# A window-attention kernel: the first pair's key shift from half its keys, copies on ScalarE at the end, another order

## The chip, the cores and the metric

The kernel runs on one core of a Trainium2 chip. The core has a matrix engine (TensorE, PE in the profile, with its weight loads as PEld), VectorE (DVE), ScalarE (ACT), GpSimd (POOL) and SyncE (SP), which here only issues transfers. The matrix engine writes to PSUM, eight banks of 128 partitions x 512 floats; everything else lies in SBUF. The metric is the time of one execution on the device in microseconds; lower is better.

## The reference

x is an image of 224 x 224 positions with 96 channels. Queries, keys and values come from one product; the channels are then cut in two halves of 48. The first half attends within 28 horizontal stripes of 8 rows, the second within 28 vertical stripes of 8 columns, 1,792 positions each. The output product joins both.

```python
qkv = jnp.einsum('bhwc,cd->bhwd', x, wqkv)
q, k, v = (qkv[..., :C], qkv[..., C:2 * C], qkv[..., 2 * C:])
scale = C2 ** (-0.5)                                  # C2 = 48
qh = q[..., :C2].reshape(B * nh, sw * W, C2)          # kh, vh alike
ah = _softmax(jnp.einsum('bqc,bkc->bqk', qh, kh) * scale, axis=-1)
oh = jnp.einsum('bqk,bkc->bqc', ah, vh).reshape(B, H, W, C2)
# qv, kv, vv: the other half, x transposed into vertical stripes; ov alike
o = jnp.pad(oh, (..., (0, C2))) + jnp.pad(ov, (..., (C2, 0)))
return jnp.einsum('bhwc,cd->bhwd', o, wo)
```

So 56 stripes need 1,792 x 1,792 scores each, an exponential of each score, and a product with the values.

## The kernel before

Two stripes make a pair; 28 pairs are worked one after the other, 14 horizontal and then 14 vertical. One stripe of a pair lies on partitions 0 to 63 and the other on 64 to 127, so that their small products run side by side. A pair has four chunks of queries (512, 512, 512, 256) and 14 tiles of 128 keys. One tile is 128 keys x 512 queries of both stripes, 1,024 columns in two PSUM banks.

Most tiles are of kind A: PE makes the scores (`qk_fn`, line 697), ScalarE takes one exponential of 128 x 1024 (line 867), and PE multiplies with the values (`pv_fn`, line 723), adding up the chunk in one bank. There are 1,126 such tiles. They use two pairs of banks in turn, so the scores of a tile wait for the exponential two tiles before. The other 246 tiles (kinds P and R) get a polynomial exponential instead: PE makes a score product (line 710), DVE and POOL work on it, PE makes the product a second time, and DVE joins the two. The remaining four banks (`RING`) serve these, the sums, and the fills: small products for keys, queries and values of the next pair, and for the output.

Softmax doesn't change when all keys are shifted by one vector, and the kernel takes a mean key off every key to keep the scores in range. For the first pair that shift is made ahead: `t_lead` turns x with PE transposes, the evictions to SBUF add up each quarter's x on the way (`xs_sb`), `kb_fn` multiplies the sums with the key weights, `kb_d` makes the shift `kb_sb`, and the evictions of the first pair's keys (`k_ev`) add it. Later pairs do it through an extra column of the query weights.

The order is written out by hand, or rather found ahead of time: `ORDER` is a string for each pair, and every letter is one item of PE's program. `q` is the score of an A tile with its exponential on ScalarE (`do_q`), `v` a product with the values (`do_v`), `1` and `3` the first and `2` and `4` the second score of a polynomial tile (`do_s`), `k` a fill for a pair ahead, `g` an output product, `f` one of the last pair's final products (`do_fill`); `K` and `G` are two fills in one. The first letters run after the lead, which is laid out by `lead_pe` and `lead_ev`. A planner (`tm` and the constants at the head of the file) walks through the letters with assumed durations, and from its times it decides which DVE, POOL and DMA step goes next; PE and ScalarE follow the letters. `emit` then writes each engine's list with its semaphore waits. Every engine works its list in order.

Names that come up below: `spin` puts filler matmuls on a zero tile into PE's list up to a time; `NTWICE` makes the scores of the first tiles twice, as filler; `XR1` and `XR2` are the times at which the planner expects the transposed x of the second and third pair; `emit_ot` copies a chunk's sums to SBUF; `out_fills` are the output products of a pair (letter `g`), `fin_fills` those of the last pair (`f`: a product, a reciprocal of the sums and a multiply-add for each 96 columns, lines 611, 618 and 623); `store` sends finished rows to the output by the queue of SP, ACT or POOL, whichever is free first by the planner's account. The lead transposes for stripe w and half hf of x, in two quarters h2:

```python
for w, hf, bs in ((0, 0, (6, 7)), (1, 0, (2, 3)), (0, 1, (6, 7)), (1, 1, (2, 3))):
    for h2 in range(2):
        f = t_lead(w, hf, h2)
        lead_pe(f, bs[h2])
        lead_ev(f, bs[h2], 0, h2 == 1)      # True: evicted by ScalarE
```

Of the kernel before, what the change touches and what calls it, by code (L numbers as in the profile page):

```python
# [32 lines left out]
D_ST, D_SW, D_TAIL = 1.0, 0.60, 1.0  # L33
XR1, XR2, TURN = 19.5, 43.0, 4.5
# [5 lines left out]
NTWICE = 11  # L40
# [5 lines left out]
    "kkqqkkq3q3q3qkqkqkqkq1q1qvvq4qkvqkv4qkqvv1qkvqvqvvq4vqkvvqkvq1vqvvq1vkqvkq4vqkvq1vqv2qvkqkqvkq2vvq3qvvvqvkq2vqvvkq",  # L46
    "1qvvvqvq2vvq1qvvqvvq3vvqvvqvkqkvqvKqvvq4qvkvq2qvvq2vqv1qvvqvqv1qvvvq4qvkvq3qvkq2vqv2qvq3vqkvqvvqkq4vqvvq4vqkvq3vqkvvqk",
    "v2qvqv1qvvvvq1qvvvvqvq3vvqvq3kqqvvqvkq4vkqq2vkqv1qkvqvvq4qvkvq3qkvqvkq2qvvq4vqkvq1vvq2qvvkq2qvv1qvvqvvqkvqvvkq1vqv2qvvq",
    "1vq2qvvq1vvqvqvvvqv1qvq1vvqvqvq4qkvq1vqvvqvq2vqv1qvv4qkqvv1qvqvkq2vqkvvq2vkqvkq3vqkqvvvqv1qvq4vqkq3vqkvq4vqvkvq4vqkvq2vk",
    "qvq1vvqvvqv2qvq1vq2qvvvqv2qvvq1qvvvqvvq1qvvqvkvqvkq1qvkqvkvq4vqvvq1qv2qkvqkv1qvvqkvqq2vqkvq1qkvvq2qvvvq1qkkqvvq2vkqvv1",  # L50
    "qvqvvqv2qvvq1vvqvv1qvvqvqv2qq4vqvkq1vqvvvqvq1vqkvkqkvvq2kqv3qkvqv4qvvqkq1vqvvvqkqvv4qvqkv2qvvq2vqv1qvq4vqvvqkvkvq1qkvvq2v",
    "vq1qvvqvvq1vvqvq1vqvvqvv3qvvqvvqvkq2qv1qvqkv2qkvqvq2vvq1qkvvvq2kqq4vqvkq1vvqkqvvq4qkvqv1qvq4vkqvq3vkqvvq3qkvqvvqvvkvq",
    "2qvv1qvvq2vq3qvvqvvqvvq1vqvvvqkqvkvq1qvvkqv2qkvqv2qkvvq1vqv4qvkqvvq2vq4qvvkq1qvkvqvvqv2qvvq2qvv3qvkqv1qvvqkvq4vqvkvq4qvvvkq1",
    "qvvqvvq2vvqvvq1vq2qvvvq1qvvqvq1vkqvvqvkqvkqv2qkvqv2qkq1vqvvq2vqv2qvkvqkq1vqv1qvqvvvqv1qkqvvvq1qkvq2qvkqv2qvvvq1kqvvqk",
    "vqvvq2vvq4qvvvvq1vqvvq4qvkq1qvvqvvvq2vqv1qvvqvkqvkqvvvq2q1qvvq1vvqkvq2vkqv3qkvqvvqvqkq4vqkq3vqvvq4vqkvqk2qvvq1vqvvkq2qkv",
    "vq1vvqvqvvvqv2qvvq1vqvkqkvkqv4qvqvk1qkqvvqv2qvq1vkqvqvvvqv4qvqkq3vqkvq3vqvvq4vqkvq2vqv1qvvqkqvvvqv3qkvqv2qvq1vkqvq2vqv2",
    "qvv1qvqvvvqvv2qvq1vvq1qvvqv1qvqvvq3qvvqvkkqkvq4qkvqv4qkvqv2qvvqv2qvvq3vqvkq1qvvqvkq4qvkqv1qvvvq2qkvqv1qvv2qvkqvkvq2qvk",
    "vvq1qkvvvqvvqvq1vqv2qvvvq1qvvqvvq1qvvqv4qkqvv3qkvqkq2vqv4qvkqvq2vvq1qvv2qkqv3qvkqvvvqkvq4qkvvq4qvvvq1qkvqkvkq2qvvq1vkqvv",
    "1qvqvvvq1qvvq1vqvvqvvq2qvv2qq2vqvvkq1qvkvqvvqv3qqvk2qvvqkvq1qv2qvvqv1qkvqkvqvvq2vqv3qvkqv4qvkqv3qvvqkq2vvqkkqvkvq1qvv",
    "vqvq1vvq2qvvq2vqv2qvvvvq3qvvvkq4qvvkvq1qvvvvqvv1qkvqv2qvqkvvq2kqv1qvvqvvvq2qvkqkkvq4qkvvqv3qvkqvvq1vqv1qkvqvvqvkvvq2qvvq1vgvvqq2vvvq",  # L60
    "vv1qvq4vqvkqvkq1vqgvqvvqv4qvvkq2qvvq1vvkqv1qkvq2qvvkqvgvq2qvvgvq1qvvgqvvvqv1qvqkq4gqvgvq3qvkq4qvvgq1qkvqvvkqvqvkgqv2qvq2vqvkvv",
# [113 lines left out]
def bass_standalone__window_attn_cswin__vision_kernel(  # L175
# [10 lines left out]
    CA = C2 + 1  # L186
# [17 lines left out]
    with es:  # L204
# [15 lines left out]
        xs_sb = sb("xs_sb", [C, 2, 4], BF16)  # L220
        kbj = sb("kbj", [128, 4], FP32)
# [410 lines left out]
        def out_fills(P):  # L632
# [3 lines left out]
            for k0 in range(0, 2 * NKT, FS):  # L636
# [16 lines left out]
                fills.append(fill("B", D_G * n, pe_fn, ["wo6"] + [("ocT", b, y) for y in range(z + 1)],  # L653
                                  [(0.07 + 96 * n * 0.001026, d, [], ["add"] if last else [("og", b, k0)], None, st)],
# [84 lines left out]
        def t_lead(w, hf, h2):  # L739
# [8 lines left out]
            acc = xs_sb[0:C, w, 2 * hf + h2:2 * hf + h2 + 1]  # L748
# [6 lines left out]
            def d(e, bk):  # L755
                dst, src = views(bk)
                return e.tensor_scalar(dst, src, 1.0, None, ALU.mult, ALU.add, accum_out=acc)

            def da(e, bk):
                dst, src = views(bk)  # L760
                return e.activation(dst, src, ACTF.Copy, accum_out=acc)
            return fill("B", 0.21, pe_fn, [("x", w, hf), "ident"],
                        [(0.6, d, [], [("xT", 0, w, hf, h2), ("xs", w, hf, h2)], da)], [], ("T", 0, w, hf) + (() if h2 else (0,)))

        def kb_fn(e, bk):
            for w in range(2):
                ins = e.matmul(bk[64 * w:64 * w + 64, 0:4], lhsT=w_sb[0:C, wblk(0, "k"), :], rhs=xs_sb[:, w, :], start=True, stop=True)
            return ins

        def kb_d(e, bk):  # L770
            return e.tensor_scalar(kbj[:, :], bk[:, 0:4], -alpha / NTOK, None, ALU.mult, ALU.add, accum_out=kb_sb[:, :])
        HH = [(hf, h2) for hf in range(2) for h2 in range(2)]
        KB = fill("B", 0.07, kb_fn, ["w", "w0z"] + [("xs", w, hf, h2) for w in range(2) for hf, h2 in HH],
# [48 lines left out]
        spin(S.done[("dve", S.cnt["dve"] - 1)])  # L822
        spin(S.done[("dve", S.cnt["dve"] - 1)], 128)
# [41 lines left out]
        def emit_qk(tl, s, slot):  # L865
            S.commit("pe", 0.0, D_MM, L_MM, qk_fn(tl, s, 2 if 1 <= ia[0] <= NTWICE else 1), kt_keys(tl), set_keys(s), fresh=set_keys(s))
# [27 lines left out]
        def store(st, done):  # L894
            if st:
                for item in st[5]:
                    q = "sp"
                    if ia[0] >= len(act_seq):
                        tm["aq"] = max(tm["aq"], tm["act"])
                        if max(done, tm["aq"]) < max(done, tm["sp"]):  # L900
                            q = "aq"
                    if ip[0] == len(p_seq) and not pq and not nq and all(d["what"] != "rn" for d in dq):
                        tm["gq"] = max(tm["gq"], tm["pool"])
                        if max(done, tm["gq"]) + D_SW < max(done, tm[q]) + D_TAIL and i2[0] == len(p_seq):
                            q = "gq"
                    tm[q] = max(done, tm[q]) + (D_SW if q == "gq" else D_TAIL if st[5][0][0] in (NP - 2, NP - 1) else D_ST)
# [104 lines left out]
        tm = dict(pe=8.43, act=7.83, end=0.0, dve=8.74, pool=11.6, sp=0.0, aq=0.0, gq=0.0, mode="B", run=9, fin=False)  # L1011
        set_free = [8.05, 7.4]
        bank_free = dict(zip(RING, (8.89, 7.98, 6.3, 6.6)))
# [5 lines left out]
        k_t = {(0, 0): 8.6}  # L1019
        q_t = {(0, 0): 7.98}  # L1020
# [3 lines left out]
        x_t = {0: 7.4, 1: XR1, 2: XR2}  # L1024
# [200 lines left out]
        def do_q():  # L1225
# [7 lines left out]
            tw = D_MM if 1 <= ia[0] <= NTWICE else 0  # L1233
# [54 lines left out]
        def do_v():  # L1288
# [163 lines left out]
```

## Time and profile before

| what | value |
|---|---|
| runs | 1055.43, 1056.22, 1056.88 us (median 1056.22) |
| the profiled execution: time, span | 1057.54 us, 1055.7 us |
| PE busy | 1027.3 us (97%) |
| ACT busy | 1041.8 us (99%) |
| DVE busy | 1014.0 us (96%) |
| POOL busy | 985.1 us (93%) |

Span is the time from the first to the last instruction of the profile. In the rows, the first two numbers of a timeline row are the start in us from the span's start and the length of the merged instructions; then come engine, line, operation, what is written and read with shapes, and how many. What stands in brackets is idle time of the engine just before and what ended it. In a row of a group, the numbers after the bar are busy time and mean ns of one, and after the second bar the idle time before them with what ended most of it. `SPq`, `ACTq` and POOL's DMA rows are issues of transfers.

### The profile page before, as it was taken

The numbers are of one execution on the slowest core, as the hardware profiler recorded it, in microseconds if no ns is written. First come the engines' busy times: TensorE is split into PE (matmuls) and PEld (weight loads), VectorE is DVE, ScalarE is ACT, GpSimd is POOL, SyncE is SP. The second block draws the span as 40 slices with busy tenths as digits, with TensorE's granted clock in tenths as the row PEclk, the third lists the DMA queues.
The fourth block names the chain that finished last, engine by engine and source line by source line (L and its number), as shares of the span: only waits on it lengthen the run. The fifth ranks groups of instructions, "written<-read, shape, count | busy, mean of one in ns | idle before, by whom it ended". The sixth has DMA issues, their size and how long they took to land.

```text
span 1055.7 us, 32757 instructions
## 1 busy us (share of the span) xinstructions
PE 1027.3 (97%) x13456; PEld 385.9 (37%) x13456; DVE 1014.0 (96%) x1748; ACT 1041.8 (99%) x1137; POOL 985.1 (93%) x654
## 2 busy tenths in 40 slices
PE   9999999999999999999999999999999999999998
PEld 4333333333333333333333433434333333333343
DVE  7989999999999999999999999999999999999998
ACT  7999999999999999999999999999999999999997
POOL 7999999999988998999999999988999999999997
PEclk9999999999999999999999999999999999999999
DMA  9867527654752854222176545537634553674352
GB/s 191 171 133 140 102 51 145 112 96 89 141 94 56 143 104 74 36 59 55 30 77 92 81 91 101 92 52 109 96 64 82 88 91 67 101 100 52 66 75 69
DMA packets 413079, 96.84 MB, mean 92 GB/s; under 512 B 403648, under 2 KB 410016, under 8 KB 412928
## 3 DMA queue, kind: packets, MB, share of 16 engines
q1 hardware_dynamic: 412080, 93.66, 51.8%
q8 instruction: 105, 1.72, 0.7%
q0 software_dynamic: 448, 0.69, 0.2%
q10 hardware_dynamic: 400, 0.39, 0.1%
q14 instruction: 46, 0.38, 0.1%
HBM read 28.31 MB, written 28.21 MB: 54 GB/s over the span
## 4 chain that ended last, share of the span: by engine, by line
PE 54%; ACT 22%; DVE 10%; POOL 7%; issue 6%; DMA 0%; ACTq 0%; POOLq 0%; DVEq 0%
ACT PT L867 22%; PE ps L723 20%; PE ps L697 20%; PE ps L710 7%; DVE PT L994 3%; POOL PT L1002 3%; PE ps L530 3%; DVE qb L989 3%; POOL PT L1005 2%; PE ps L575 1%; POOL PT L1006 1%; PE ps L644 1%; DVE PT L991 1%; DVE og L650 1%; DVE V_sb L582 1%
## 5 line engine op out<-in xcount | busy, mean ns | idle before, releaser
L867 ACT ACTIVATE PT<-ps 128x1024 bf16<-128x1024 f32 x1126 | 1037.2, 1080 | 4.1 <-PE ps L697 2.9
L1002 POOL TENSOR_TENSOR PT<-PT 128x1024 f16<-128x1024 f16 x246 | 461.8, 1894 | 20.3 <-DVE PT L991 11.3
L697 PE MATMUL ps<-QT_sb,KT_sb 49*64 49x512 bf16 (+1 forms) x5332 | 461.6, 362 | 15.9 <-ACT PT L867 9.7
L723 PE MATMUL ps<-PT,V_sb 128*49 128x512 bf16 (+1 forms) x3136 | 464.4, 361 | 0.0
L994 DVE SCALAR_TENSOR_TENSOR PT<-ps,PT 128x512 uint16<-128x512 f32 (+1 forms) x405 | 312.4, 799 | 15.7 <-PE ps L710 6.8
L989 DVE TENSOR_SCALAR qb<-ps 128x512 f16<-128x512 int16 (+1 forms) x421 | 313.7, 775 | 11.9 <-PE ps L710 7.8
L1005 POOL TENSOR_TENSOR PT<-qb 128x1024 f16<-128x1024 f16 x150 | 283.2, 1894 | 22.9 <-DVE qb L989 10.8
L697 PEld LDWEIGHTS ps<-QT_sb,KT_sb 49*64 49x64 bf16 x5332 | 135.4, 104 | 308.3 <-ACT PT L867 284.2
L723 PEld LDWEIGHTS ps<-PT,V_sb 128*49 128x49 bf16 x3136 | 134.2, 103 | 205.7 <-issue 173.5
L710 PE MATMUL ps<-QT_sb,KT_sb 50*64 50x512 bf16 (+1 forms) x1968 | 196.6, 390 | 5.3 <-DVE PT L994 1.2
L1006 POOL TENSOR_SCALAR PT<-PT 128x1024 f16<-128x1024 f16 x150 | 156.9, 1046 | 12.8
L991 DVE SCALAR_TENSOR_TENSOR PT<-ps,qb 128x512 f16<-128x512 int16 (+1 forms) x172 | 123.0, 743 | 0.2
L710 PEld LDWEIGHTS ps<-QT_sb,KT_sb 50*64 50x64 bf16 (+1 forms) x1968 | 55.8, 103 | 76.3 <-DVE PT L994 22.9
L884 DVE CAST OT_sb<-ps 113x512 bf16<-113x512 f32 x112 | 68.9, 615 | 0.5 <-PE ps L723 0.4
L544 DVE CAST QT_sb<-ps 128x512 bf16<-128x512 f32 (+1 forms) x111 | 67.0, 614 | 1.7 <-PE ps L530 1.0
L535 DVE TENSOR_SCALAR_CACHE_REDUCE KT_sb<-ps 128x512 bf16<-128x512 f32 x106 | 63.8, 617 | 1.3 <-PE ps L530 0.8
L650 DVE CAST og<-ps 128x480 bf16<-128x480 f32 x84 | 51.4, 617 | 1.4 <-PE ps L644 0.7
L582 DVE CAST V_sb<-ps 128x480 bf16<-128x480 f32 (+1 forms) x84 | 51.3, 616 | 0.4 <-PE ps L575 0.4
L530 PE MATMUL ps<-xT_sb,w_sb 97*64 97x512 bf16 x224 | 41.9, 371 | 0.3 <-DVE qb L989 0.2
L530 PE MATMUL ps<-xT_sb,wq_sb 97*64 97x512 bf16 x224 | 40.8, 367 | 0.1
L575 PEld LDWEIGHTS ps<-w_sb,xT_sb 96*64 96x64 bf16 x1568 | 33.5, 112 | 16.1 <-issue 7.1
L575 PE MATMUL ps<-w_sb,xT_sb 96*64 96x48 bf16 x1568 | 39.1, 190 | 0.0
(66 smaller groups left out, 248.6 us busy)
## 6 DMA issues: line engine op xcount, KB each, us to landing
xT_sb<-xt_dram SPq DMA_DIRECT2D x28, 336.0 KB, 5.2
xp_dram<-in_x_dram SPq DMA_DIRECT2D x26, 336.0 KB
oc_all<-xp_dram SPq DMA_DIRECT2D x26, 336.0 KB, 3.6
xt_dram<-xT_sb SPq DMA_DIRECT2D x26, 336.0 KB, 6.5
out_dram<-og SPq DMA_DIRECT2D x181, 48.0 KB, 2.0
oh_all<-ohn SPq DMA_DIRECT2D x52, 84.0 KB, 2.8
stg<-oh_all SPq DMA_DIRECT2D x13, 336.0 KB, 6.0
xt_dram<-xT_sb SPq DMA_DIRECT2D x4, 168.0 KB, 4.6
```

What stands on the lines that cost most here:

```text
L530: ins = e.matmul(bk[64 * w:64 * w + 64, 0:qs], lhsT=lw, rhs=xT_sb[b][0:C + 1, w, q0:q0 + qs], start=True, stop=True)
L575: ins = e.matmul(bk[64 * h:64 * h + 64, j * C2:(j + 1) * C2], lhsT=xT_sb[b][0:C, w, t0:t0 + 64], rhs=w_sb[0:C, wblk(P, "v"), 0:C2], start= ...
L697: ins = e.matmul(bank(SETS[s] + w)[64 * kh:64 * kh + 64, i * t["qs"]:(i + 1) * t["qs"]], lhsT=KT_sb[b][64 * w:64 * w + CA, kt * 128 + 64 * ...
L710: ins = e.matmul(bank(bp[w])[64 * kh:64 * kh + 64, 0:512], lhsT=KT_sb[b][64 * w:64 * w + nr, kt * 128 + 64 * kh:kt * 128 + 64 * kh + 64], ...
L723: ins = e.matmul(bank(pb)[64 * w:64 * w + CA, 0:t["qs"]], lhsT=V_sb[b][:, w, kt, :], rhs=PT[slot][:, ca:ca + t["qs"]], start=st and i == 0 ...
L867: S.commit("act", 0.0, D_ACT, None, lambda e, s=s, slot=slot: e.activation(PT[slot][:], ps[:, 512 * SETS[s]:512 * SETS[s] + 1024], ACTF.Ex ...
L989: fn, reads, writes = lambda e: e.tensor_scalar(q, l, m, a, ALU.mult, ALU.add), bk, qk
L991: fn, reads, writes = lambda e: e.scalar_tensor_tensor(y.bitcast(FP16), l, -RA * 2.0 ** 16, q, ALU.add, ALU.mult), bk + qk, ptk
L994: fn, reads, writes = lambda e: e.scalar_tensor_tensor(y.bitcast(U16), f, 128.0, y.bitcast(FP16), ALU.mult, ALU.add), bk + ptk, ptk
L1002: square = ("pool", D_SQ, lambda e: e.tensor_tensor(y, y, y, ALU.mult), yk + ["pser"], yk)
L1005: return [("pool", D_SQ, lambda e: e.tensor_tensor(y, q, q, ALU.mult), qk, yk), ("pool", D_AF, lambda e: e.tensor_scalar(y, y, -(QS * (RB ...
L1006: ("pool", D_AF, lambda e: e.tensor_scalar(y, y, -(QS * (RB + RA) / 2) ** 2, 1.0, ALU.add, ALU.mult), yk + ["pser"], yk),
```

## The change

Three parts, and a new order.

The lead. Only the first half of each stripe of the first pair (hf = 0) adds up into the shift; the second half's evictions are plain copies. The shift's product has two columns instead of four for each stripe, and the factor is doubled. PE's lead list changes: transposes of three of the four halves, first queries, shift product, first keys, and then the transposes of the last half; before, it was all four halves, queries, keys, shift product. ScalarE evicts the first quarter of that last half and DVE the second. The filler behind the lead is gone, and the expected landing times of x, up to which the filler ahead of the lead runs, are 0.6 to 0.9 us later. The scores are made twice for tiles 3 to 11 instead of 1 to 11, and ORDER begins with `qqkk` in place of `kkqq`.

The end. Once the last exponential is laid out, ScalarE copies what a `g` product gives, and it copies the sums of the very last chunk. Both were DVE's. The planner's account of the output queues changes too.

The order. All 28 strings of ORDER and the planner's starting times are new. The counts of `q` and `v`, the tiles and their kinds stay.

```diff
-D_ST, D_SW, D_TAIL = 1.0, 0.60, 1.0
-XR1, XR2, TURN = 19.5, 43.0, 4.5
+D_ST, D_SW, D_END = 1.0, 0.60, 0.60
+XR1, XR2, TURN = 20.05, 43.5, 4.5
-NTWICE = 11
+NTW0, NTWICE = 3, 11
+CT = 9.5
 ORDER = [
-    "kkqqkkq3q3q3qkqkqkqkq1q1qvvq4qkvqkv4qkqvv1qkvqvqvvq4vqkvvqkvq1vqvvq1vkqvkq4vqkvq1vqv2qvkqkqvkq2vvq3qvvvqvkq2vqvvkq",
...
-    "qvvv1qvvq2vqv1qvvqvvvqgvqv1qvgqgvvq1qvvvgq2qvvq2vqv1qvvvqvvqvq4vqgvq4vqvgvq3fqvvvq4vfqvvq3vqvvqvvqvgq4vfqvvq2vfqvqgvqgffqvvvfqfqfvvfqfvvvgvvfff",
+    "qqkkqkkq1qkq3qkqk3q1qqvq1qkqvv2qvqkvkvq2qkvqkvq3qvkvqvqvkq2kvq1qvkqkq1qvvvqkqvkq1vvq2qvvvq4qvkvq4vqkvq3vqvvvq4qkvvvq1",
...
+    "qvv1qvvq1qvvvqvvqv1qgvqv2qvvvq1vqv2qvvq2vqv1qvvqgvvqvqvgqv1qvvfqv2qvvq2vvq2qvvvffqvqv3qvvfqvvqvvq4vfqvvq2vqvffqvvvfqgqvvfqfvgqvgvvffvgff",
 ]
...
-                    x_lead[w][:, hf * FTH * C:(hf + 1) * FTH * C], f"x{w}{hf}", land=3.4 + 1.0 * hf + 0.3 * w)
+                    x_lead[w][:, hf * FTH * C:(hf + 1) * FTH * C], f"x{w}{hf}", land=4.02 + 1.25 * hf + 0.25 * w)
...
+                def da(e, bk, k0=k0, n=n):
+                    return e.activation(rows[:, k0:k0 + n, :], bk[:, 0:n * C].rearrange("p (s c) -> p s c", s=n), ACTF.Copy)
...
-            acc = xs_sb[0:C, w, 2 * hf + h2:2 * hf + h2 + 1]
+            acc = xs_sb[0:C, w, h2:h2 + 1]
...
             def d(e, bk):
                 dst, src = views(bk)
+                if hf:
+                    return e.tensor_scalar(dst, src, 1.0, None, ALU.mult)
                 return e.tensor_scalar(dst, src, 1.0, None, ALU.mult, ALU.add, accum_out=acc)
             def da(e, bk):
                 dst, src = views(bk)
+                if hf:
+                    return e.activation(dst, src, ACTF.Copy)
                 return e.activation(dst, src, ACTF.Copy, accum_out=acc)
...
-            return e.tensor_scalar(kbj[:, :], bk[:, 0:4], -alpha / NTOK, None, ALU.mult, ALU.add, accum_out=kb_sb[:, :])
+            return e.tensor_scalar(kbj[:, :], bk[:, 0:2], -2.0 * alpha / NTOK, None, ALU.mult, ALU.add, accum_out=kb_sb[:, :])
...
-        for w, hf, bs in ((0, 0, (6, 7)), (1, 0, (2, 3)), (0, 1, (6, 7)), (1, 1, (2, 3))):
+        for w, hf, bs in ((0, 0, (6, 7)), (1, 0, (2, 3)), (0, 1, (6, 7))):
...
         lead_pe(Q[0], 5)
+        lead_pe(KB, 0)
         lead_pe(K[0], 4)
         lead_ev(Q[0], 5, 0, True)
-        lead_pe(KB, 0)
         lead_ev(KB, 0)
         lead_ev(K[0], 4, 0)
         lead_ev(K[0], 4, 1)
-        spin(S.done[("dve", S.cnt["dve"] - 1)])
-        spin(S.done[("dve", S.cnt["dve"] - 1)], 128)
+        for h2 in range(2):
+            f = t_lead(1, 1, h2)
+            lead_pe(f, 6 + h2)
+            lead_ev(f, 6 + h2, 0, h2 == 0)
...
-            S.commit("pe", 0.0, D_MM, L_MM, qk_fn(tl, s, 2 if 1 <= ia[0] <= NTWICE else 1), kt_keys(tl), set_keys(s), fresh=set_keys(s))
+            S.commit("pe", 0.0, D_MM, L_MM, qk_fn(tl, s, 2 if NTW0 <= ia[0] <= NTWICE else 1), kt_keys(tl), set_keys(s), fresh=set_keys(s))
...
+                    d_t = D_ST
                     if ia[0] >= len(act_seq):
+                        d_t = D_END
+                    if pv_open[0] >= len(pv_chunks):
                         tm["aq"] = max(tm["aq"], tm["act"])
...
+                if (P, c) == (NP - 1, NCH - 1):
+                    tm["act"] = max(tm["act"], st + L_PV) + 0.41
...
+                    S.commit("act", 0.0, 0.41, 0.51, lambda e, b0=acc[0]: e.activation(
+                        OT_sb[P % 2][0:64 + CA, q0:q0 + qs], bank(b0)[0:64 + CA, 0:qs], ACTF.Copy),
+                        [("bank", acc[0])], [("OT", P % 2, c)])
...
+            if c == "g" and ia[0] >= len(act_seq):
+                z = f["chain"][0]
...
+                S.commit("act", 0.0, z[6], z[6] + 0.1, lambda e, fn=z[4], bk=bank(b[0]): fn(e, bk), [("bank", b[0])] + z[2], z[3])
+                store(z, done)
```

More of the change, by code (lines that the diff above doesn't have):

```diff
@@ L50 @@
[L50 to L61, printed above, removed]
@@ L219, in bass_standalone__window_attn_cswin__vision_kernel @@
         warm = sb("warm", [128, 512], BF16)
-        xs_sb = sb("xs_sb", [C, 2, 4], BF16)
-        kbj = sb("kbj", [128, 4], FP32)
+        xs_sb = sb("xs_sb", [C, 2, 2], BF16)
+        kbj = sb("kbj", [128, 2], FP32)
         kb_sb = sb("kb_sb", [128, 1], FP32)
@@ L1010, in bass_standalone__window_attn_cswin__vision_kernel @@
         NB = len(RING)
[L1011 to L1013 removed]
+        tm = dict(pe=7.45, act=7.85, end=0.0, dve=8.2, pool=11.2, sp=0.0, aq=0.0, gq=0.0, mode="B", run=9, fin=False)
+        set_free = [6.65, 5.8]
+        bank_free = dict(zip(RING, (7.7, 7.15, 7.95, 8.3)))
         busy = set()
```

77 lines of the change are left out of this document (52 added, 25 removed).

## The prediction, made before the change was run

> **What bounds the kernel now.** I read the page's head and groups first, then the exponential's own rows, then the first 11 us and the last 6 us in the timeline.
>
> ```profile
> span 1055.7 us, 32757 instructions
> ...
> PE 1027.3 (97%) x13456; PEld 385.9 (37%) x13456; DVE 1014.0 (96%) x1748; ACT 1041.8 (99%) x1137; POOL 985.1 (93%) x654
> ...
> L867 ACT ACTIVATE PT<-ps 128x1024 bf16<-128x1024 f32 x1126 | 1037.2, 1080 | 4.1 <-PE ps L697 2.9
> ...
> L697 PE MATMUL ps<-QT_sb,KT_sb 49*64 49x512 bf16 (+1 forms) x5332 | 461.6, 362 | 15.9 <-ACT PT L867 9.7
> ...
> L710 PE MATMUL ps<-QT_sb,KT_sb 50*64 50x512 bf16 (+1 forms) x1968 | 196.6, 390 | 5.3 <-DVE PT L994 1.2
> ```
>
> ScalarE (ACT) is the belt: 1,126 exponentials of 128x1024, one after the other, idle for 4.1 us in all. The row of its line gives the first and the last start:
>
> ```profile
> L867 ACT ACTIVATE PT<-ps x1126: 1017/1070/1292, 10.7 to 1048.8; 128x1024 bf16<-128x1024 f32 x188
> ```
>
> So the time splits in three: a lead of 10.7 us before the first exponential, 1038.0 us from the first start to the last (1,125 steps of 0.923), and 6.9 us from the last start to the end of the span. The run of this profile took 1057.54 us, 1.8 more than its span and 1.3 more than the median of 1056.22; I make the sum as differences and put them on the median.
>
> ACT has next to no holes, yet its step is 0.923 where the most frequent one is 0.904. The reason is TensorE (PE), which works in the order of ORDER. Its rows around one long stretch:
>
> ```profile
> 344.42 0.41 PE L697 MATMUL ps<-QT_sb,KT_sb 49*64 49x512 bf16 x4
> 344.75 1.06 PE L723 MATMUL ps<-PT,V_sb 128*49 128x512 bf16 x14
> 345.74 0.41 PE L697 MATMUL ps<-QT_sb,KT_sb 49*64 49x512 bf16 x4
> ```
>
> Four `v` between two `q` take 1.32 us from score to score, more than one exponential lasts. I paired all 1,125 steps with the number of PE items between the two scores in ORDER: with none or one the mean step is 0.912 (282 of them), with two 0.910 (554), with three 0.946 (250), with four or more 1.028 (39). So the body's time is a matter of how ORDER spreads its long stretches.
>
> **The lead.** The three engines that make it, each in order of time:
>
> ```profile
> 4.04 3.22 PE L745 MATMUL ps<-ident,oh_all 112*96 112x112 bf16 x32 [0.37 <-DMA oh_all<-in_x_dram]
> 7.19 0.64 PE L530 MATMUL ps<-xT_sb,wq_sb 97*64 97x512 bf16 x2
> 7.62 0.64 PE L530 MATMUL ps<-xT_sb,w_sb 97*64 97x512 bf16 x2
> ...
> 8.07 0.29 PE L767 MATMUL ps<-xs_sb,w_sb 96*64 96x4 bf16 x2
> ...
> 9.16 1.06 PE L530 MATMUL ps<-xT_sb,w_sb 97*64 97x512 bf16 x2
> 10.15 0.94 PE L697 MATMUL ps<-QT_sb,KT_sb 49*64 49x512 bf16 x12
> ```
>
> ```profile
> 5.80 0.54 ACT L761 ACTIVATE xT_sb<-ps 96x448 bf16<-96x448 bf16 x1
> 6.24 0.19 ACT L761 ACTIVATION_READ_ACCUMULATOR xT_sb<-ps 96x1 bf16 x1
> ...
> 7.87 0.60 ACT L547 ACTIVATE QT_sb<-ps 128x512 bf16<-128x512 f32 x1
> 10.72 1.02 ACT L867 ACTIVATE PT<-ps 128x1024 bf16<-128x1024 f32 x1 [2.26 <-PE ps L697]
> ```
>
> ```profile
> 8.44 0.16 DVE L771 TENSOR_SCALAR_CACHE_REDUCE kbj<-ps 128x4 f32<-128x4 f32 x1 [0.89 <-PE ps L372]
> 8.52 0.08 DVE L771 DVE_READ_ACCUMULATOR kbj<-ps 128x1 f32 x1
> 8.64 0.88 DVE L778 TENSOR_SCALAR KT_sb<-ps,kb_sb 128x128 bf16<-128x128 f32 x2
> ```
>
> PE turns x (32 transposes at 0.10 each), makes the first queries, the first keys and the shift, fills until the shifted keys are in SBUF, makes two more blocks of keys (`kk`), and only then the first scores. ACT waits 2.26 us for them.
>
> After the change, with these durations:
> - Filler: one matmul of 512 columns (0.43, the distance of 7.19 and 7.62) and two of 128 (0.11 each) more. Cover: the wait for x, 0.37 idle. They overrun it by about 0.1; if x lands earlier they cost up to 0.3.
> - 24 transposes before the queries instead of 32: 4.1 + 24 x 0.10 = 6.5. The fourth eviction, the last that the queries need, ends at 6.24 + 0.19 = 6.43 already now. Queries at 6.55.
> - Shift product at 6.98 (0.43 later), keys at 7.14 (its two products took 0.15 to the next filler), the other 8 transposes 7.57 to 8.37. DVE has the shift by 7.5, so it is hidden, and the first 128 keys about 0.3 after the keys' own end at 7.78: 8.1. ACT's query eviction: 7.2 to 7.8.
> - First scores at 8.37 (behind the transposes on PE), since ORDER now begins with `qq`; their exponential 0.57 later, as 10.15 to 10.72: 8.94 instead of 10.72, that is **1.8 us** earlier.
> - Late next: the other 384 keys leave DVE at 8.7, so the second scores are ready by 9.4, before ACT is free at 9.85. The last turned quarter leaves DVE at 9.3; `kk` follows, 0.85 at this rate, the third scores at 10.2 and their exponential at 10.8 against ACT free at 10.75: nothing to speak of. The accumulator reads of the second half fall away (0.19 each on ACT, 0.08 on DVE), off this path. The doubled scores go from 11 to 9, beside ACT.
> - Bounds: at least 1.0 (one more 0.43 matmul and a late quarter in the way), at most 2.2. SP's queue keeps its order of issues here; the planner only expects x of the second pair 0.5 later.
>
> **The body.** The new ORDER has the same 1,126 `q`, 1,372 `v`, and 1,914 instead of 1,919 changes between scores and 128-row products. Between two `q` stand none or one item 306 times (282), two 514 times (554), three 262 times (250), four or more 43 times (39). With the means above: 24 x 0.912 - 40 x 0.910 + 12 x 0.946 + 4 x 1.028 = +0.95 us. One of the four extra long ones is `vvvff`, whose `f` are products of 97 columns, so I take **+0.8**. What the counts don't show are waits of PE for others than ACT: 15.9 - 9.7 = 6.2 before scores, 5.3 before the polynomial's. A new order can meet fewer or more of these 11.5 us; a quarter either way is 2.9, and my bounds for the body are -2.1 and +3.7.
>
> **The tail.** The engines from the last exponential on:
>
> ```profile
> 1050.28 0.65 ACTq L291 DMA_DIRECT2D out_dram<-og  x1
> 1050.31 0.42 DVE L884 CAST OT_sb<-ps 113x256 bf16<-113x256 f32 x1
> ...
> 1050.79 0.29 PE L611 MATMUL ps<-wov,OT_sb 49*64 49x97 bf16 x8 [0.32 <-DVE OT_sb L884]
> ...
> 1051.49 0.97 DVE L623 SCALAR_TENSOR_TENSOR og<-ps,rc,og 128x96 bf16<-128x96 f32 x4
> 1051.79 0.55 POOL L291 DMA_DIRECT2D out_dram<-og  x1 [0.67 <-DVE og L623]
> 1052.53 1.09 POOL L291 DMA_DIRECT2D out_dram<-og  x2 [0.19 <-DVE og L623]
> ```
>
> ```profile
> DMA to landing us min/median/max: 1.8/2.0/2.3
> ```
>
> Last start 1048.8; last eviction of sums 1.5 to 1.9 after it; DVE done 3.7 after; two stores one behind the other on POOL (0.55 each); end 6.9 after. In the new tail ACT takes a copy of 480 columns (about 0.56, by the 0.60 for 512) as soon as its last exponential has issued, then the last sums (0.42 to 0.60), then 288 columns. The first is over at 1.5, just when the sums' product is: no delay, but also little gain. DVE loses three copies, yet the last products still can't start before 2.0, and the last reciprocals and 4 sums (0.25 + 0.97) end at 3.4 to 3.6. The final rows go out on SP, ACT and POOL rather than twice on POOL: 0.55 less at most, against up to 0.5 more where a queue's store lands in 2.3 instead of 1.8. I take **-0.3**, bounds -0.8 and +0.4.
>
> **Sum.** -1.8 + 0.8 - 0.3 = -1.3: the profiled execution's 1057.54 becomes 1056.2, and the median 1056.22 becomes **1054.9**.
>
> **Rule and row.** Two products of 512 columns start 0.43 apart at 7.19 and 7.62. The twelve scores of the same width from 10.15 on run four side by side, in three groups; 0.94 less one group's 0.41 leaves 0.27 from start to start. So PE goes from about half its rate to the full one near 10.3. The Trainium skill (TensorE: Matmul & The Clock Gate, Part 1: The HAM clock gate) has the gate open after a busy free-running window of about 3.4 us, and Part 4 (PE-mode transpose) says that transposes don't count as busy. The trace agrees: full rate came some 3 us behind the first product after the transposes. By that rule the 8 transposes that now stand among the products can leave the gate shut for one window more, to about 13.6; that is the second rival.
>
> **Rivals.**
> 1. The new order meets fewer of the 11.5 us of waits, or the lead starts the belt 2.2 earlier: with a quarter of the waits gone, 1054.9 - 2.9 = 1052.0 at the far end, about 1053.3 typically. For: the order was laid out for the new start. Against: its counts are no better. Chance 0.38 for all below 1054.1.
> 2. Half rate lasts 3.4 us longer, to 13.6. A doubled score then takes 0.86 and a polynomial's 0.43, 1.3 with one of each against a step of 0.91; three such steps lose 1.2 and the next two fills 0.4: 1056.5. For: transposes among the products. Against: the ones now stood in one block and the rate rose anyway. Chance 0.12, with the other ways of ending within 0.8 of no change.
> 3. Slower: the new order puts polynomial scores ahead of buffers that DVE and POOL have not yet freed (the 5.3 and 6.2 us). PE then stands still while ACT drains its two score buffers. If these waits grow by 40%, +4.6: 1059.5. It decides from 3.4 us more of such waits than I count on. For: DVE 96% and POOL 93% leave little slack. Against: ACT's own idle is 4.1 now. Chance 0.10 for all above 1058.3.
> 4. The tail does not shorten, because the last DVE step ends at the same place and the store only changes its queue: 1055.2, inside the forecast.
>
> **Numbers.** 0.2% is 2.1 us, about what a measurement of this kernel can tell from no change. My forecast, a gain smaller than that, holds 0.40, rival 2 0.12, rival 1 0.38, rival 3 0.10: faster 0.38, same 0.52, slower 0.10. The range reaches to half of rival 1 and past rival 2: 1052.4 to 1057.4.
>
> **What would show it.** First exponential at 8.9 (8.5 to 9.7), with ACT's wait before it near 0.2 to 0.5 and no hole before the third; the step between exponentials 0.922 to 0.925; from the last exponential to the end 6.4 to 7.0. The lead is wrong if the first scores wait for DVE's keys or PE's half rate goes past 10.5; the body if the distance from first to last exponential leaves 1036 to 1041.7; the tail if ACT's copy of 480 columns holds up the last sums.

## The result: 1213.5 us, and the profile after

The changed kernel takes 1213.51 us (1208.94 to 1215.02), the kernel before in the same runs 1055.97 (1055.43 to 1056.88): a ratio of 1.1483, interval 1.1461 to 1.1504. The forecast was 1054.9. The profiled execution took 1214.25 us. The changed kernel's page, its head and the groups of the exponential and of the product that fills make for queries:

```profile
span 1212.5 us, 32733 instructions
...
PE 1081.7 (89%) x13448; PEld 393.3 (32%) x13448; DVE 1016.9 (84%) x1739; ACT 1051.7 (87%) x1138; POOL 983.7 (81%) x650
...
ACT  8597999779699868987999999588998869578998
...
PEclk9797999789799889988999999798999879798999
...
L877 ACT ACTIVATE PT<-ps 128x1024 bf16<-128x1024 f32 x1126 | 1046.1, 1069 | 153.0 <-PE ps L701 138.0
...
L531 PE MATMUL ps<-xT_sb,wq_sb 97*64 97x512 bf16 x224 | 43.4, 383 | 106.2 <-DMA xT_sb<-xt_dram 59.5
```

The work is the same; ScalarE is idle before exponentials for 153.0 us instead of 4.1, and it waits for scores. PE's row of granted clock (`PEclk`, 9 where it is 90% or more of the full clock) is below 9 in 15 slices, and in each of them ScalarE's row is below 9 too. In these traces the granted clock is either full or half; below, the gate is called open or shut for that. The last row names the cause: before the query products PE is idle for 106.2 us, nearly all of it for transfers into `xT_sb` (59.5 and, in the list of waits below, 46.5). The exponential's own rows split the time as the prediction did:

```profile
L877 ACT ACTIVATE PT<-ps x1126: 1018/1062/1237, 8.4 to 1206.3; 128x1024 bf16<-128x1024 f32 x188
```

| part of the span, us | before | after | with the late transfers entered later (first experiment) |
|---|---|---|---|
| to the first exponential (lead) | 10.72 | 8.38 | 8.46 |
| first to last start (body) | 1038.03 | 1197.96 | 1038.74 |
| last start to the end (tail) | 6.96 | 6.12 | 6.12 |
| span | 1055.7 | 1212.5 | 1053.3 |

So lead and tail went as meant, and the body grew by 159.9 us. The waits by engine, line and releaser (us in total, times, longest):

```profile
ACT PT L877 <- PE ps L701: 138.0, 78, 14.7
...
PE ps L531 <- DMA xT_sb<-xt_dram: 59.5, 9, 9.4
...
PE ps L531 <- DMA xT_sb<-oc_all: 46.5, 8, 13.8
```

There are seventeen such waits of PE, and ScalarE's trace has exactly seventeen steps from one exponential to the next of more than 3 us, 3.03 to 15.74. Each lies at the second or third tile of its pair. They hold 115.7 us beyond the step of 0.904 that is most frequent. The first of them, on PE, and on the queue of SP that issues the transfer:

```profile
45.45 0.41 PE L701 MATMUL ps<-QT_sb,KT_sb 49*64 49x512 bf16 x4
59.66 0.42 PE L531 MATMUL ps<-xT_sb,wq_sb 97*64 97x256 bf16 x2 [13.79 <-DMA xT_sb<-oc_all]
59.84 1.52 PE L727 MATMUL ps<-PT,V_sb 128*49 128x512 bf16 x6
61.29 0.64 PE L701 MATMUL ps<-QT_sb,KT_sb 49*64 49x512 bf16 x4
```

```profile
44.25 3.52 SPq L292 DMA_DIRECT2D xt_dram<-xT_sb  x2
...
54.18 3.15 SPq L409 DMA_TRANSPOSE xT_sb<-oc_all  x2
```

The product waits until a transfer has landed that SP only issues at 54.2, after all that stands ahead of it in its queue. The code says why. At the first `q` of pair P, `do_q` calls `queue_prep(P + 1)`, and this enters into the planner's books the transfer that brings the x of pair P + 2. There are two buffers of x, so it is written where the x of pair P lies. The books let a reader wait for the latest write that has been entered. A query fill of pair P (a `k`, line 531) that stands in ORDER *behind* its pair's first `q` therefore waits for the x of pair P + 2. The old ORDER has no such fill; the new one has 20, in 19 pairs, one to six letters late. In pairs 26 and 27 nothing is left to bring, and there the trace shows no stop; the other 17 pairs are the 17 stops. (These queries, the last 256 of a pair and once 512 more, are then made from the x of two pairs later, so for the 17 pairs the changed kernel does not compute what the reference asks.)

Beyond the stops 65 steps of over 1.2 us hold 46.4 us more. They stand behind the stops, where the clock is half for a while; the remaining steps are 2.2 us shorter in sum than before. ScalarE's exponentials by windows (length, busy time and number, granted clock, DMA share, GB/s):

```profile
59.60:64.10 4.50, 1.94 (x2) 0.50 1.10 200
64.10:68.70 4.60, 3.90 (x5) 0.95 0.80 147
```

Four matmuls of 512 columns now take 0.64, where they took 0.41, and two exponentials pass in 4.5 us.

The theory then: 20 letters stand behind the point where their buffer is given away; 17 of them stop PE, and a stop shuts PE's clock gate as well. Rivals: the change to the lead or the tail costs the time, or the new order itself does, by its spread of scores.

### The profile page after: what moved, and what is told of

Same layout as the page of the kernel before. It is cut to its first block, busy times and chain, and to the rows that moved or that the text cites. A ratio compares the mean times of both kernels' runs of the same rounds, so it can differ in the third digit from the quotient of the medians.

```text
span 1212.5 us, 32733 instructions
## 1 busy us (share of the span) xinstructions
PE 1081.7 (89%) x13448; PEld 393.3 (32%) x13448; DVE 1016.9 (84%) x1739; ACT 1051.7 (87%) x1138; POOL 983.7 (81%) x650
## 4 chain that ended last, share of the span: by engine, by line
PE 58%; ACT 17%; DVE 7%; DMA 7%; SPq 4%; issue 4%; POOL 2%; ACTq 0%; DVEq 0%; POOLq 0%
PE ps L727 23%; PE ps L701 20%; ACT PT L877 16%; PE ps L714 8%; DMA xT_sb<-xt_dram 4%; DMA xT_sb<-oc_all 4%; SPq L292 3%; PE ps L531 3%; DVE qb L1004 2%; DVE PT L1009 2%; PE ps L576 2%; PE ps L645 1%; SPq L409 1%; DVE KT_sb L536 1%; POOL PT L1020 1%
## 5 line engine op out<-in xcount | busy, mean ns | idle before, releaser
L877 ACT ACTIVATE PT<-ps 128x1024 bf16<-128x1024 f32 x1126 | 1046.1, 1069 | 153.0 <-PE ps L701 138.0
L701 PE MATMUL ps<-QT_sb,KT_sb 49*64 49x512 bf16 (+1 forms) x5324 | 479.5, 377 | 14.2 <-ACT PT L877 9.5
L727 PE MATMUL ps<-PT,V_sb 128*49 128x512 bf16 (+1 forms) x3136 | 491.7, 382 | 0.3 <-DVE KT_sb L934 0.3
L701 PEld LDWEIGHTS ps<-QT_sb,KT_sb 49*64 49x64 bf16 x5324 | 138.2, 105 | 311.1 <-ACT PT L877 255.1
L727 PEld LDWEIGHTS ps<-PT,V_sb 128*49 128x49 bf16 x3136 | 140.7, 106 | 230.4 <-issue 190.2
L714 PE MATMUL ps<-QT_sb,KT_sb 50*64 50x512 bf16 (+1 forms) x1968 | 206.3, 409 | 4.6 <-DVE PT L1009 0.9
L531 PE MATMUL ps<-xT_sb,wq_sb 97*64 97x512 bf16 x224 | 43.4, 383 | 106.2 <-DMA xT_sb<-xt_dram 59.5
L531 PEld LDWEIGHTS ps<-xT_sb,wq_sb 97*64 97x64 bf16 x224 | 13.1, 111 | 122.3 <-issue 70.3
L981 POOL TENSOR_TENSOR stg<-OT_tr,rn 128x768 bf16<-128x768 bf16 (+1 forms) x26 | 34.1, 1312 | 10.1 <-PE ps L727 5.9
```

The source lines that it names most:

```text
L531: ins = e.matmul(bk[64 * w:64 * w + 64, 0:qs], lhsT=lw, rhs=xT_sb[b][0:C + 1, w, q0:q0 + qs], start=True, stop=True)
L701: ins = e.matmul(bank(SETS[s] + w)[64 * kh:64 * kh + 64, i * t["qs"]:(i + 1) * t["qs"]], lhsT=KT_sb[b][64 * w:64 * w + CA, kt * 128 + 64 * ...
L714: ins = e.matmul(bank(bp[w])[64 * kh:64 * kh + 64, 0:512], lhsT=KT_sb[b][64 * w:64 * w + nr, kt * 128 + 64 * kh:kt * 128 + 64 * kh + 64], ...
L727: ins = e.matmul(bank(pb)[64 * w:64 * w + CA, 0:t["qs"]], lhsT=V_sb[b][:, w, kt, :], rhs=PT[slot][:, ca:ca + t["qs"]], start=st and i == 0 ...
L877: S.commit("act", 0.0, D_ACT, None, lambda e, s=s, slot=slot: e.activation(PT[slot][:], ps[:, 512 * SETS[s]:512 * SETS[s] + 1024], ACTF.Ex ...
```

## The experiments

**The transfers entered after the fill.** ORDER and all else stay as changed; where the last query fill of pair P is still to come, the books enter the later transfer only behind it (`bring_x` holds the lines taken out).

```diff
-            if 2 <= P < NPH - 1:
-                turn_x(P + 1)
...
-            elif P >= NPH - 1 and P + 1 < NP:
-                plan_x(P + 1)
+            if any(f["gives"][:2] == ("Q", P - 1) for f in prep_q):
+                behind[P - 1] = P
+            else:
+                bring_x(P)
...
+            if g[0] == "Q" and g[2] == NCH - 1 and P in behind:
+                bring_x(behind.pop(P))
```

> The changed kernel with its ORDER untouched; where a pair's last query fill stands behind the pair's first q, the transfers of x for the pair two later (turn, load, keep, block, or the plain load in the second half) are entered behind that fill. Theory A: the fills find their own x, PE's waits for xT_sb vanish, 1053 to 1058 us; the transfers start some 2 us later, which their distance to the next pair's keys should hide. Theory B or C: 1190 us or more.

Measured: 1055.12 us (1054.72 to 1055.22), before 1055.21, ratio 0.9993 (0.9984 to 1.0002). (A ratio here and below is taken over all the runs of both kernels, so it need not be that of the two medians.) Its exponential's group, and PE at the place of the first stop:

```profile
L885 ACT ACTIVATE PT<-ps 128x1024 bf16<-128x1024 f32 x1126 | 1037.4, 1077 | 2.6 <-PE ps L701 1.0 <-DVE rn L974 0.3 <-issue 0.2
```

```profile
45.45 0.41 PE L701 MATMUL ps<-QT_sb,KT_sb 49*64 49x512 bf16 x4
45.79 0.30 PE L531 MATMUL ps<-xT_sb,wq_sb 97*64 97x256 bf16 x2
45.92 0.81 PE L727 MATMUL ps<-PT,V_sb 128*49 128x512 bf16 x6
```

The fill that started at 59.66 starts at 45.79, and ScalarE's idle time is 2.6 us. All 158 us are gone with the same order, lead and tail, so those are not the cause. This is what the change is worth when its fills read the x they were meant to: nothing that can be measured.

**The letters put ahead.** The 20 late `k` are moved directly ahead of their pair's first `q`; the code stays.

```diff
-    ...vvvq4qkvvvq1",
+    ...vvvq4kqvvvq1",
```

> The changed kernel with one thing different: the 20 letters k in ORDER that fill a pair's last queries after that pair's first q now stand directly ahead of that q, one to six letters earlier. Theory A (a query fill behind its pair's first q waits for the transposed x that the transfer queue brings for the pair two later, because that transfer is entered in the program's books at the first q): the waits of PE for xT_sb, 150 us in the changed kernel, fall to near none, and the time to 1053 to 1056 us. Theory B (the new order as a whole, or the lower granted clock of 0.92, makes the time): little changes, 1190 us or more. Theory C (ScalarE's copies at the end or the new lead): 1213 us.

Measured: 1071.13 us (1070.85 to 1071.41), ratio 1.0147 (1.0132 to 1.0161), at a granted clock of 1.00. The groups:

```profile
L877 ACT ACTIVATE PT<-ps 128x1024 bf16<-128x1024 f32 x1126 | 1043.1, 1068 | 13.0 <-PE ps L701 9.5 <-POOL PT L1017 0.2
...
L714 PE MATMUL ps<-QT_sb,KT_sb 50*64 50x512 bf16 (+1 forms) x1968 | 197.7, 392 | 15.6 <-DVE PT L1009 5.6 <-DVE PT L1006 2.0 <-DVE QT_sb L545 1.7
```

No wait for `xT_sb` is left, which bears the theory out: 142 us are gone. The other 16 I had not expected. PE's waits before the polynomial's scores are 15.6 us instead of 5.3, mostly for DVE, and the lag grows pair by pair. Twenty letters, moved by one to six places, cost an order that was fitted to its own DVE and POOL steps 1.5%. Which of them, and by which DVE step, is open.

**The same fault put into the kernel before.** In pairs 4, 8, 12, 18 and 22 the last `k` of the pair goes from ahead of the first `q` to directly behind it (those queries read the x of two pairs later).

```diff
-    "...vqvkvq4vqkvq2vk",
-    "qvq1vvqvvqv2...
+    "...vqvkvq4vqkvq2vq",
+    "kvq1vvqvvqv2...
```

> The kernel before with one thing different: in five pairs (4, 8, 12, 18, 22) the letter k of the last query fill is put directly behind the pair's first q. In these pairs the last 256 queries are then made from the x of two pairs later, as in the changed kernel. Theory A: five waits of about 9 us (157 us over 17 pairs in the changed kernel), 1100 us within 15, and the granted clock below 1. Theory B or C: 1056 us.

Measured: 1098.71 us (1096.6 and 1100.82), ratio 1.0407 (1.0386 to 1.0428), clock 0.974. PE's waits:

```profile
PE ps L530 <- DMA xT_sb<-xt_dram: 16.0, 3, 9.7
...
PE ps L530 <- DMA xT_sb<-oc_all: 6.7, 2, 4.2
```

Five letters, five stops (steps of 5.59, 4.10, 2.96, 11.67 and 5.91 us). The body grows by 39.3 us, of which the stops hold 25.7; the rest lies behind them. So one letter moved by one place makes a step of 3 to 12 us where one of 0.9 stood, with nothing else of the change there.

**The stops kept, the gate held open.** The changed kernel, with 7 to 66 filler matmuls of 512 columns ahead of each of the 17 waiting fills, into the bank that the fill writes next.

```diff
+            if c == "k" and P in begun and g[0] == "Q":
+                for _ in range(STOP.pop(P, 0)):
+                    S.commit("pe", 0.0, D_MM, D_MM + 0.2, lambda e, bk=bank(b[0]): e.matmul(
+                        bk[0:64, :], lhsT=warm[:, 0:64], rhs=warm[:, :], start=True, stop=True),
+                        ["warm"], [("bank", b[0])])
```

> The changed kernel with filler matmuls of 512 columns on a zero tile ahead of each of the 17 late query fills that wait for a transfer, 7 to 66 of them, about 1.5 us less than each stop lasted. They go to the bank that the fill then overwrites; the fill itself still waits for x. Theory gate (65 slower steps behind the stops, 46 us of the 160, are PE at half rate because the stop shut its clock gate): the stops stay, the steps behind them return to about 0.92, 1165 to 1185 us, granted clock above 0.98. Theory refill (the steps are slow because sums and polynomial tiles have to catch up): 1205 to 1220 us.

Measured: 1167.12 us (1167.09 and 1167.16), ratio 1.1058 (1.1038 to 1.1079), clock 0.999. ScalarE behind the first stop, in the changed kernel and then in this one:

```profile
61.98 1.94 ACT L877 ACTIVATE PT<-ps 128x1024 bf16<-128x1024 f32 x2 [14.73 <-PE ps L701]
64.80 1.94 ACT L877 ACTIVATE PT<-ps 128x1024 bf16<-128x1024 f32 x2 [0.88 <-PE ps L701]
```

```profile
61.53 4.69 ACT L878 ACTIVATE PT<-ps 128x1024 bf16<-128x1024 f32 x5 [14.18 <-PE ps L702]
```

The stop stays, and behind it five exponentials pass without a hole. Over the whole run the seventeen steps still hold 111.6 us (115.7 in the changed kernel), while of the 65 longer steps behind them five are left, with 1.9 us instead of 46.4. So about 45 us of the 157.5 are half rate behind the stops, 2.6 for each, and the other 111 or so are the waits. The Trainium skill (TensorE: Matmul & The Clock Gate, Part 1: HAM oscillation) says that waits for DMA longer than the activity window shut the gate again each time. The trace agrees: the clock was 0.50 behind a wait of 13.79 us. Shorter waits did it too: in the changed kernel a stretch of half clock begins in or just behind 16 of the 17 waits, also one of 2.62 us (0.50 from 392.3 to 402.5), and only the one of 2.10 us has none.

**The old order in the new code.** The changed kernel with all 28 strings of ORDER as before; the first begins with `kkqq`.

```diff
-    "qqkkqkkq1qkq3qkqk3q1...
+    "kkqqkkq3q3q3qkqkqkqk...
```

> The changed kernel with the strings of ORDER of the kernel before (its planner starts from the new times). Theory A: none of these strings has a late query fill, so 1053 to 1056 us, the lead's 2.3 us less some loss where the old strings do not fit the new start. Theory C (lead or ScalarE's copies): 1200 us or more.

Measured: 1064.73 us (1060.24 to 1065.22), ratio 1.0073 (1.0056 to 1.0089). Its windows (the last three numbers of a row: granted clock, DMA share, GB/s):

```profile
8.00:12.00 4.00, 2.63 (x46) 1.13 (x50) 3.34 (x7) 2.23 (x4) 3.71 (x6) 0.91 1.44 190
12.00:16.00 4.00, 4.00 (x52) 1.65 (x48) 3.38 (x3) 3.23 (x4) 3.02 (x3) 0.50 0.82 183
16.00:20.00 4.00, 4.00 (x48) 1.20 (x43) 2.95 (x4) 2.58 (x3) 3.75 (x4) 0.50 0.94 228
20.00:25.00 5.00, 5.00 (x42) 1.52 (x38) 3.26 (x5) 3.65 (x4) 5.00 (x4) 0.50 0.98 156
25.00:30.00 5.00, 4.32 (x48) 1.28 (x50) 3.62 (x6) 4.64 (x6) 4.84 (x4) 1.00 0.94 163
```

The two `kk` ask at 8.8 for the quarter of x that is now turned last and wait 1.14 us for DVE's copy, PE works 2.63 of 4 us, and from 12 to 25 us it has half its clock though it is busy throughout. Against the profile of before, the exponentials fall back by 4.8 us in the first 25 us, and by as much again, at full clock, up to the ninth pair; then the order runs as before. I had expected 1053 to 1056. So half the loss comes at full clock, if behind the shut gate. The old strings therefore don't suit the new lead; that `kk` ahead of `qq` alone makes the difference is likely, and not shown. What is shown is that without a late fill there is no stop: the longest wait of PE from there on is under 1 us, and none is for `xT_sb` from a transfer.

**Less filler ahead of the lead.** The repaired kernel of the first experiment with the landing times of before: one filler of 512 columns and two of 128 fewer.

```diff
-                    ..., land=4.02 + 1.25 * hf + 0.25 * w)
+                    ..., land=3.4 + 1.0 * hf + 0.3 * w)
```

> The changed kernel with the transfers entered behind the late fills (turn_behind), and the filler ahead of the transposes ending where it did in the kernel before (one matmul of 512 and two of 128 columns fewer). If it is the filler up to the landing of x that opens the gate at 6.6 us or earlier: the first product behind the transposes runs at 0.43 instead of 0.21 a matmul, the first exponential starts at 8.9 to 9.2 instead of 8.4, 0.5 to 1.5 us more in all (1055.6 to 1056.6). If not: 1055.1.

Measured: median 1054.49 us, ratio 1.0011 (0.9988 to 1.0034): eight of ten runs lie within 1054.37 to 1054.92, the other two at 1063.66 and 1065.01. The profile is of the last. Its exponentials by windows, then PE in it, and the repaired kernel's window:

```profile
12.00:37.00 25.00, 17.74 (x19) 1.00 0.97 174
```

```profile
30.99 0.64 PE L701 MATMUL ps<-QT_sb,KT_sb 49*64 49x512 bf16 x4
```

```profile
12.00:37.00 25.00, 24.94 (x29) 1.00 1.02 180
```

In these 25 us, in which PE was never idle, four scores take 0.64 instead of 0.41, half the rate, and ScalarE has 19 exponentials instead of 29. The column of the granted clock prints 1.00 all the while, but it is made from the clock records of the trace (stretches of full or half clock, each with its start and length) and prints 1.00 also where there is none. Here the first record, of the full clock, begins at 37.56 us; the same four scores take 0.64 at 35.8 and 0.41 at 37.7. So the gate stayed shut until then. The other long run has no profile. Less filler is not the whole cause: the kernel before has as little of it, and none of its 27 runs beside these is above 1056.88. Why the gate stays shut for so long under load is open.

**The kernel before once more.** No edit.

> The kernel before, unchanged, for a second profile. Its times fall in two groups, near 1055.0 and near 1056.7. If PE's clock gate opens at different times in the lead, the first exponential starts at 10.5 to 10.8 in the slower group and 1 us or more earlier in the faster one, with body and tail the same. If the groups come from elsewhere, the first start stays at 10.5 to 10.8.

Measured: 1056.31 us (1054.53 to 1058.44). In this profile:

```profile
4.02 2.85 PE L745 MATMUL ps<-ident,oh_all 112*96 112x112 bf16 x32 [0.35 <-DMA oh_all<-in_x_dram]
6.80 0.41 PE L530 MATMUL ps<-xT_sb,wq_sb 97*64 97x512 bf16 x2
```

The first exponential starts at 9.12 instead of 10.72: PE has its full rate at the first queries (0.41; 0.64 in the profile I predicted from). The first clock record of the full clock begins at 5.88 us here and at 10.41 there. The body is 1038.42, the tail 6.96. So 1.6 us of the start differ between two executions of one kernel; this one took 1056.31 us, the one I predicted from 1057.54. The ratio of this kernel to its own copy is 1.0009 (0.9999 to 1.002): a difference of one part in a thousand can come without any change.

**The end alone, and the end with the filler.** The kernel before with the change's lines for the end, ScalarE's copies and the queue account:

```diff
+                if (P, c) == (NP - 1, NCH - 1):
...
+            if c == "g" and ia[0] >= len(act_seq):
...
```

Then the same with the changed landing times, and the filler behind the lead as many matmuls long as in before:

```diff
-                    ..., land=3.4 + 1.0 * hf + 0.3 * w)
+                    ..., land=4.02 + 1.25 * hf + 0.25 * w)
...
-        spin(S.done[("dve", S.cnt["dve"] - 1)])
-        spin(S.done[("dve", S.cnt["dve"] - 1)], 128)
+        spin(S.done[("dve", S.cnt["dve"] - 1)] - 0.43)
+        spin(S.done[("dve", S.cnt["dve"] - 1)] - 0.43, 128)
```

> The kernel before with the change's end alone: ScalarE copies the last output product and the last chunk's sums, and the new account of the output queues. Tail from the last exponential's start 6.1 to 6.5 us instead of 6.96; body and lead as before; 0.4 to 0.8 us less than the kernel before. If the tail came from the new ORDER instead: no change.

> The kernel before with the change's end and with the change's filler ahead of the transposes (one matmul of 512 and two of 128 columns more), ORDER and lead otherwise as before. If the filler makes the gate open the same way each time, the groups of tail_only (1054.7, 1056.2, 1057.5) become one, at 1054.5 to 1055.2, some 0.3 to 1 us less than the kernel before. If not, the groups stay.

Measured: 1055.31 us (1054.67 to 1057.76), ratio 1.0007 (0.9998 to 1.0016), with a tail of 6.16 us instead of 6.96; and 1056.25 us (1055.03 to 1057.52), ratio 1.0007 (0.9998 to 1.0016), with a tail of 6.12. The end brings 0.8 us in the profile, less than the 3.1 and 2.5 us over which the runs of these two kernels spread, and neither kernel's time is below that of before. I expected more filler to take that spread away, and it did not.

**Two small fillers fewer.** The repaired kernel with `land=3.82`, two fillers of 128 columns less.

```diff
-                    ..., land=4.02 + 1.25 * hf + 0.25 * w)
+                    ..., land=3.82 + 1.25 * hf + 0.25 * w)
```

> turn_behind with two 128-column filler matmuls fewer ahead of the transposes (0.2 us; between turn_behind and short_filler). If filler up to the landing of x keeps the gate from staying shut through the first 30 us: all times within 1 us of each other, as in turn_behind (1054.7 to 1055.2), and not in two groups 10 us apart as in short_filler (eight of ten near 1054.5, two near 1064); median 1054.5 to 1055.1. If it was chance: a group above 1060 can show here too.

Measured: 1054.44 us (1053.96 to 1054.58), before 1055.48, ratio 0.9989 (0.998 to 0.9998).

```profile
3.94 1.72 PE L749 MATMUL ps<-ident,oh_all 112*96 112x112 bf16 x24
...
6.02 0.41 PE L531 MATMUL ps<-xT_sb,wq_sb 97*64 97x512 bf16 x2 [0.20 <-POOL wq_sb L340]
```

The first exponential comes at 7.75; in this execution the full clock begins at 3.79, ahead of the transposes. The time is lower than that of before by about one part in a thousand, no more than the unchanged kernel differed from its copy, so a gain is not shown. The eleven runs lie within 0.7 us, as the ten of the repaired kernel do, where those of before spread over 1.9 us; no long run came.

## Why the prediction was wrong

*The step that failed* is **The body**. It took the new order as a sequence of PE items, counted how many stand between two scores, and reckoned +0.8 us, with +3.7 as its upper bound. It never asked of a moved fill which write its read would then follow, and it looked at SP's queue for the lead only. The waits that it allowed for are more or fewer of those that PE had before (11.5 us), and rival 3, the one on the slower side, has polynomial scores wait for buffers that DVE and POOL free. Instead PE stopped for x, at other letters: seventeen steps hold 115.7 us and the half rate behind them 46.4, of a body that grew by 159.9. The order of letters could have told it: the pair's first `q` against its last `k`, 0 late ones before and 20 after, since in `queue_prep` the transfer is entered at once. The kernel before showed no such wait because it has no such letter, so its trace could not have bounded it.

*The counting itself held.* With the late transfers out of the way the body took 1038.74, 0.71 us more than before where +0.8 was reckoned, and inside the limits named. The waits that the counts don't show (11.5 us before) came to 10.4. That the two numbers agree so closely is in part luck: the body was 1037.78 to 1038.42 in four profiles with the old order in the old code, and 1038.74 and 1038.33 in the first and the last experiment, so a gain or loss of 0.8 hardly stands out. (The range's lower end, 1052.4, lies near the far end of rival 1 and not at half of it, as the prediction says; nothing here hangs on it.)

*The lead* was right in its mechanism and mis-sized in one term, PE's rate. The changed kernel's rows:

```profile
4.24 2.47 PE L749 MATMUL ps<-ident,oh_all 112*96 112x112 bf16 x24
...
6.74 0.41 PE L531 MATMUL ps<-xT_sb,wq_sb 97*64 97x512 bf16 x2
...
7.92 0.93 PE L701 MATMUL ps<-QT_sb,KT_sb 49*64 49x512 bf16 x8
```

Transposes start at 4.24 instead of 4.1 and take 0.10 each, and the queries are 0.2 late; then the scores come at 7.92 instead of 8.37, since PE was at its full rate from 6.6 and not from about 10.4. First exponential 8.38 (8.46 repaired) instead of 8.94: 2.3 us won against that profile, not 1.8, and past the bound of 2.2. Against the other profile of before, which starts at 9.12, it is 0.7. In three further profiles with the old lead (the two of the end and that of the fault put in) it starts at 9.00, 9.22 and 10.49. I took one execution's gate for the kernel's.

*Rival 2* (half rate for 3.4 us longer, by transposes among the products) did not come in the changed kernel: the products at 6.74 take 0.41. The Trainium skill (TensorE: Matmul & The Clock Gate, Part 4: PE-mode transpose) says that transposes don't count as busy in the same way. No run here tells it for certain, since 2.7 to 3.3 us of filler run ahead of them. The clock records fit it: the changes of the clock within a trace lie whole multiples of 3.41 us apart, and in the profile that I predicted from the stretch of 3.41 us up to 7.00, with 3.0 us of transposes and hardly any filler, did not open the gate, while the next one did, at 10.41. In the changed kernel the stretch up to 6.56, with 1.1 us of filler and 2.3 of transposes, opened it. The same page's Part 1 has a window that runs free of the program and an onset that differs from run to run; the two profiles of before agree (full clock at 5.88 and at 10.41). What the rival describes, a gate that stays shut longer, did come with less filler, at 10 us instead of 1.6.

*The tail* had the right parts and too small a sum: -0.84 where -0.3 stood and -0.8 was the limit. The end of the repaired kernel on ScalarE and on DVE:

```profile
1048.11 0.64 ACT L654 ACTIVATE og<-ps 128x480 bf16<-128x480 f32 x1
1048.78 0.38 ACT L1337 ACTIVATE OT_sb<-ps 113x256 bf16<-113x256 f32 x1
1049.22 0.41 ACT L654 ACTIVATE og<-ps 128x288 bf16<-128x288 f32 x1
```

```profile
1049.74 0.99 DVE L624 SCALAR_TENSOR_TENSOR og<-ps,rc,og 128x96 bf16<-128x96 f32 x4
```

The last exponential starts at 1047.2, the copies take 0.64, 0.38 and 0.41, and DVE ends 3.5 after that start, within the 3.4 to 3.6 reckoned (3.7 before). From there the span has 2.6 us left, 3.2 before: the store that POOL no longer issues behind another saved its whole 0.55 and a little more, and nothing was lost on the other queues. Rival 4 falls. Rival 1 (earlier start, fewer waits) is right on the lead only; the last experiment's 1054.44 is the nearest thing to it.

## What to carry to other kernels

When the order of a program is changed under a scheduler that keeps its own books of reads and writes, compare each read not with its engine's neighbours but with the point at which the next write of its buffer is entered; a read one place behind that point waits for a transfer that belongs two stages later. Look at the DMA that a releaser names: an engine that suddenly waits for a buffer it has read all along may be reading it too late, not too early. And take the start of a kernel from more than one execution before crediting a change with a microsecond there.

## What was not expected of the hardware

- A stop of PE costs more than itself: 17 stops of 3 to 16 us cost 46 us behind them at half the rate, and with filler matmuls during the stops 1.9 of these are left (1213.5 to 1167.1 in all). Three waits of 2.2 to 2.6 us (two in the kernel before with the fault put in, one in the changed kernel) shut the gate, one of 2.1 did not. In the changed kernel the half clock began 0.9 to 4.4 us after the start of the wait, lasted one to five times 3.41 us, and outlasted the wait by 3.7 to 13.5 us.
- The gate can stay shut under load. With PE busy 5.00 of 5.00 us the clock was 0.50 from 12 to 25 us (the old order in the new code). With less filler, PE took 0.64 for four scores until 37 us in the profiled execution, and two of ten runs were 9 to 11 us longer. The granted-clock column printed 1.00 there, because the trace had no clock record yet; ahead of the first record the matmul's own length tells the rate.
- When the gate opens in the first 10 us differs from execution to execution of the same kernel: at 5.88 and at 10.41 in two profiles of the kernel before, which is 1.6 us at the first exponential.
